# Batch 0's attention with key tiles of 128 instead of 112, its values loaded by all heads at once, in a fused attention and mixer kernel

## The chip, the cores and the metric

The kernel runs on one core of one Trainium2 chip. The metric is the time of one execution on the device, in microseconds, as the median of several.

## The reference, cut to what matters

```python
# q, k, v: (batch 8, heads 12, seq 448, head_dim 64), fp32; tau = 0.1
q_n = q / (norm(q) + 1e-6);  k_n = k / (norm(k) + 1e-6)
attn = softmax(q_n @ k_n.T / tau)             # by head
x = (attn @ v), heads side by side            # (8, 448, 768)
u = x + ((x.T @ U) @ V).T                     # low-rank mixing over seq, rank 32
out = u + relu(u @ w_ch1) @ w_ch2             # 768 -> 3072 -> 768
```

Cosine similarities lie in -1..1, so the kernel leaves out the subtraction of the maximum, and it takes the sum of a softmax row from a column of ones beside v.

## The kernel before: what the change and the argument touch

A planner in Python orders the operations of all engines by estimated times and emits each engine's instructions in that order. Two consequences matter below. In the traces an instruction whose data come late holds up what stands behind it on its engine: in the run with AV late, a square waits 1.46 us for its load, and the exp behind it starts 2.35 us after its score was begun. Any edit may order the rest of the program anew.

Work goes by pairs of heads. For a pair, 448 keys and queries in 4 blocks of 112 rows are squared and reduced (norms), scaled, transposed by TensorE into PSUM, copied to SBUF (`qkT`), multiplied into scores, put through `exp` on ScalarE, and multiplied with v (AV). In batches 1 to 7 keys are tiles of 128, seven for a pair: three of head A, three of head B, and one with 64 rows of each, whose v rows hold zeros for the other head. In batch 0, whose start is in a hurry, keys stay in their blocks of 112:

```python
small = b == 0
rows_ = SCH if small else 128                      # SCH = 112
for m in range(8 if small else 7):
    ... score matmul into sc, 448 columns ...
    exps[m] = ACT exp(attn[0:rows_, m, ...] <- sc)
# AV: 16 matmuls a head either way; batch 0 reads its own value tile raw_v [112, 12, 4, 66]
...
# order of the first loads on GpSimd's queue
load_qk(0, 0, 2); load_qk(0, 2, 4); load_qk(0, 4, 8)
load_v0(0, 4)                                      # 4 loads: heads 0..3
load_qk(0, 8, 12)
load_v0(4, 8); load_v0(8, 12)
load_w1(0, 6); load_w1(6, 12)
```

`raw_v` shares its memory with w2. The two tiles for 128-row values are prepared (ones and zeros) by GpSimd at leisure. ScalarE's instructions are all activations or copies, and VectorE and ScalarE share the copies out of PSUM and the squares, as the planner finds one of them free.

## Time and profile before

| | before |
|---|---|
| time, median of the first 3 runs | 608.21 us (608.17 to 608.47) |
| time of the profiled execution | 607.15 us |
| TensorE busy | 587.7 of 605.0 us |
| TensorE idle before 40 us | 11.4 us |
| first exp, last exp of batch 0 ended | 10.74, 38.05 us |
| first MLP matmul | 39.40 us |

How to read it: from 39.4 us on TensorE is a nearly unbroken queue of matmuls. Before that it waits for the first batch, which ScalarE carries. The lines that show this stand in the prediction.

### The profile page before, as it was taken

The page shows a single profiled execution, that of the slowest core. Times are in us where ns is not written, and L with a number is a line of the kernel's source. Part 1 is how long each engine was busy: PE and PEld are TensorE (multiplying, and loading weights), DVE is VectorE, ACT ScalarE, POOL GpSimd, SP SyncE. Part 2 cuts the span into 40 slices and gives each one's busy share as a digit, 9 for nine tenths or more (in the row PEclk, how much of TensorE's full clock was granted, in tenths as well). Part 3 has the DMA queues.
Part 4 walks back from the last instruction along what each step waited for, and adds up shares of the span by engine and source line. Part 5 has one row for each costly group of instructions (what it writes and reads, how often), then busy time and mean ns, then how long its engine had stood idle before and what let it go on. Part 6 is the DMA issues. An engine that isn't in the chain of part 4 may idle for free.

```text
span 605.0 us, 11545 instructions
## 1 busy us (share of the span) xinstructions
PE 587.7 (97%) x4731; PEld 348.6 (58%) x4731; DVE 295.6 (49%) x703; ACT 281.3 (46%) x606; POOL 120.9 (20%) x191
## 2 busy tenths in 40 slices
PE   4899999999999999999999999999999999999997
PEld 2565665555555665666445665666545666654565
DVE  8979669899998899644711253015300210110011
ACT  6977752488772286327641077506442015014300
POOL 8737234062611626000600000000000000000000
PEclk9999999999999999999999999999999999999999
DMA  9999997999998999724902141030002110310021
GB/s 121 191 206 113 205 197 96 151 150 145 123 113 151 183 153 143 98 67 84 157 0 66 43 89 41 1 93 27 15 1 53 52 40 1 88 43 1 0 53 53
DMA packets 150228, 54.58 MB, mean 90 GB/s; under 512 B 115104, under 2 KB 150176, under 8 KB 150176
## 3 DMA queue, kind: packets, MB, share of 16 engines
q0 software_dynamic: 73408, 25.96, 39.0%
q1 hardware_dynamic: 76704, 27.86, 24.7%
q8 instruction: 37, 0.61, 0.4%
q14 instruction: 15, 0.12, 0.1%
q10 hardware_dynamic: 64, 0.02, 0.0%
HBM read 52.25 MB, written 11.01 MB: 105 GB/s over the span
## 4 chain that ended last, share of the span: by engine, by line
PE 92%; ACT 5%; DVE 1%; DMA 0%; issue 0%; POOL 0%; ACTq 0%; POOLq 0%
PE mm L768 36%; PE mm L734 35%; PE sc L546 9%; PE av L566 7%; ACT attn L551 3%; PE mm L658 1%; ACT qkT L798 1%; PE mm L623 1%; PE tp L371 1%; ACT sq L438 1%; DVE xn L509 1%; PE sc L734 1%; DMA qk_nat<-in_k_dram 0%; ACT uT L798 0%; PE sc L658 0%
## 5 line engine op out<-in xcount | busy, mean ns | idle before, releaser
L734 PE MATMUL mm<-uT,w_sb 128*128 128x512 bf16 (+1 forms) x1134 | 236.5, 353 | 0.0
L768 PE MATMUL mm<-w_sb,relu 128*128 128x384 bf16 (+1 forms) x1368 | 233.4, 323 | 0.3 <-ACT uT L798 0.3
L551 ACT ACTIVATE attn<-sc 128x448 bf16<-128x448 f32 (+1 forms) x342 | 164.3, 565 | 98.0 <-PE av L566 66.4
L768 PEld LDWEIGHTS <-relu 128*128 128x128 bf16 x1368 | 132.6, 98 | 86.7 <-issue 0.9
L734 PEld LDWEIGHTS <-w_sb 128*128 128x128 bf16 x1152 | 112.2, 98 | 101.2 <-issue 0.8
L757 ACT ACTIVATE relu<-mm 128x384 bf16<-128x384 f32 (+1 forms) x172 | 93.9, 546 | 149.3 <-PE mm L734 148.9
L777 DVE TENSOR_TENSOR O_sb<-mm,u_nat 128x384 f32<-128x384 f32 (+1 forms) x57 | 31.1, 549 | 229.4 <-PE mm L768 222.6
L546 PE MATMUL sc<-qkT 128*128 128x448 bf16 (+1 forms) x342 | 105.8, 358 | 4.3 <-DVE qkT L800 1.3
L566 PEld LDWEIGHTS <-attn 128*128 128x128 bf16 (+1 forms) x1536 | 62.7, 98 | 17.7 <-issue 2.3
L409 POOL DMA_DIRECT2D v_nat<-in_v_dram x98 | 63.1, 650 | 35.4 <-DMA w_sb<-in_moe_w_ch_dram 9.7
L444 DVE TENSOR_REDUCE ss<-sq 112x8 f32<-112x512 bf16 x96 | 63.2, 673 | 1.1 <-ACT sq L438 0.7
L509 DVE TENSOR_TENSOR xn<-qk_nat,inv 112x512 bf16<-112x512 bf16 (+1 forms) x97 | 62.4, 676 | 0.3
L566 PE MATMUL av<-v_nat,attn 128*128 128x65 bf16 x1344 | 55.7, 193 | 0.0
L546 PEld LDWEIGHTS <-qkT 128*128 128x128 bf16 (+1 forms) x342 | 31.9, 103 | 24.1 <-issue 7.2
L387 POOL DMA_DIRECT2D qk_nat<-in_q_dram x25 | 17.8, 713 | 134.6 <-DVE xn L509 89.5
L575 DVE TENSOR_TENSOR X_sb<-av,rd 128x256 bf16<-128x256 f32 x96 | 40.2, 419 | 1.7
L573 DVE RECIPROCAL rd<-av 128x4 f32<-128x4 f32 x96 | 17.1, 179 | 38.2 <-PE av L566 37.4
L440 DVE TENSOR_TENSOR sq<-qk_nat 112x512 bf16<-112x512 bf16 x89 | 34.6, 413 | 0.9 <-DMA qk_nat<-in_q_dram 0.8
L672 DVE TENSOR_TENSOR u_nat<-mm,X_sb 128x384 bf16<-128x384 f32 x36 | 19.0, 552 | 11.1 <-PE mm L658 10.9
L371 PE MATMUL tp<-ident,xn 112*128 112x112 bf16 x144 | 11.1, 220 | 8.0 <-DVE xn L509 7.9
L387 POOL DMA_DIRECT2D qk_nat<-in_k_dram x25 | 17.6, 702 | 3.3 <-DMA w_sb<-in_moe_w_ch_dram 3.0
L457 ACT ACTIVATE ln<-ss 112x32 f32<-112x32 f32 (+2 forms) x26 | 6.1, 235 | 23.5 <-DVE ss L444 23.5
(60 smaller groups left out, 174.9 us busy)
## 6 DMA issues: line engine op xcount, KB each, us to landing
qk_nat<-in_q_dram POOLq DMA_DIRECT2D x23, 224.0 KB, 5.7
qk_nat<-in_k_dram POOLq DMA_DIRECT2D x23, 224.0 KB, 6.8
w_sb<-in_moe_w_ch_dram POOLq DMA_DIRECT2D x4, 1152.0 KB, 13.4
w_sb<-in_moe_w_ch_dram POOLq DMA_DIRECT2D x8, 576.0 KB, 16.2
out_dram<-O_sb SPq DMA_DIRECT2D x15, 168.0 KB, 2.2
out_dram<-O_sb SPq DMA_DIRECT2D x16, 144.0 KB, 2.1
out_dram<-O_sb SPq DMA_DIRECT2D x16, 120.0 KB, 2.0
out_dram<-O_sb SPq DMA_DIRECT2D x16, 96.0 KB, 2.2
```

The lines of the kernel that those rows point to most:

```text
L387: ops = [load(lambda i=i, src=src: nc.gpsimd.dma_start(out=ld.tile[:, i, lo:lo + h1 - h0, :], in_=src[b, h0:h1].rearrange("h (s c) d -> s ...
L409: nc.gpsimd.dma_start(out=vb[p0:p0 + s1 - s0, hs, j, 0:D], in_=v[b, hs].rearrange("h (s c) d -> c s h d", c=SC)[c, s0:s1]),
L440: nc.vector.tensor_mul(y, x, x)
L444: lambda i=i, a0=a0, a1=a1, sq=sq: nc.vector.reduce_sum(ss.tile[:, i, a0:a1, :].rearrange("p h c -> p (h c)"), sq.tile[:, 0:a1 - a0, :].re ...
L509: nc.vector.tensor_mul(dst, src, sc)
L546: nc.tensor.matmul(out=sc.tile[0:rows_, 0:S], lhsT=kT[:, rows_ * m:rows_ * (m + 1)], rhs=qkT.tile[:, 8:12, :].rearrange("p c s -> p (c s)" ...
L551: exps[m] = plan.add(Op("ACT", act_t(S), lambda sc=sc, m=m: nc.scalar.activation(out=attn.tile[0:rows_, m, off:off + S], in_=sc.tile[0:row ...
L566: nc.tensor.matmul(out=av.tile[:, t, 0:D + 1], lhsT=attn.tile[0:rows_, m, 128 * t:128 * (t + 1)], rhs=vv[0:rows_, h, j, 0:D + 1], start=(j ...
L575: muls.append(plan.add(Op("DVE", dve_t(256), lambda av=av, rd=rd, h=h: nc.vector.tensor_mul(X.tile[:, :, h * D:(h + 1) * D], av.tile[:, :, ...
L734: o = plan.add(Op("PE", pe_t(n), lambda cc=cc: nc.tensor.matmul(out=mm.tile[:, 0:n], lhsT=w1_sb[:, cc, f * 128:(f + 1) * 128], rhs=uT.tile ...
L757: nc.scalar.activation(out=relu.tile[:, f, 0:n], in_=mm.tile[:, 0:n], func=AF.Relu)
L768: nc.tensor.matmul(out=mm.tile[:, 0:c1 - c0], lhsT=relu.tile[:, f, i * 128:(i + 1) * 128], rhs=w2.tile[:, f, c0:c1], start=(f == 0), stop= ...
```

## The change

Its intent: seven exps for each pair of batch 0 instead of eight, which is 6 of 48, on the engine that carries the chain. Keys come in blocks of 112 from the transposes, so tiles of 128 are put together while they leave PSUM: each of a head's first three blocks is filled up with 16 rows of the fourth, and the 64 rows that are left go to the mixed tile. Values must then lie in tiles of 128 too, and eight loads (six of all heads, two of every second head, each some rows of one block) bring them straight to that layout. w2 gets its own tile.

```diff
-    r_w2 = Ring(... "raw_v" ... then "w2_sb" in the same memory ...)
+    w2_t = const.tile([128, NC, C], BF, name="w2_sb")
+    def load_v0():                                  # all heads
+        for j in range(3):
+            part(0, SCH, slice(0, H, 1), j, j, 0)             # 112 rows of block j
+            part(SCH, 16, slice(0, H, 1), j, 3, 16 * j)       # 16 rows of block 3
+        for hh in range(2):
+            part(64 * hh, 64, slice(hh, H, 2), 3, 3, 48)      # the last 64 rows
...
+    def key_tiles(t_, x, h0, h1):                   # three copies for a block, in place of one
+        return [(full[:, :, :, 0:SCH], x[:, :, 0:3, :]),
+                (full[:, :, :, SCH:128], x[:, :, 3, 0:48] ...),
+                (t_[:, 768 + 64 * h0:768 + 64 * h1] ..., x[:, :, 3, 48:SCH])]
...
-        for m in range(8 if small else 7):
+        for m in (0, 1, 2, 6, 3, 4, 5) if b == 0 else range(7):
...
-    load_v0(0, 4)
+    load_v0()
     ld, ops, _ = load_qk(0, 8, 12)
-    load_v0(4, 8)
-    load_v0(8, 12)
...
-    v_set = [plan.add(Op("POOL", 1.5, lambda t_=t_: set_v(t_)), pool_q) for t_ in v_t]
+    v_set = [fill(lambda: set_v(v_t[0]), 1000, prio=-1.4),           # VectorE, at the start
+             fill(lambda: set_v(v_t[1]), 1000, prio=3, deps=late)]   # VectorE, late
```

## The prediction

> **What bounds the kernel now.** I read the page first: busy shares, slices, the chain that ended last.
>
> ```profile
> PE 587.7 (97%) x4731; PEld 348.6 (58%) x4731; DVE 295.6 (49%) x703; ACT 281.3 (46%) x606; POOL 120.9 (20%) x191
> PE   4899999999999999999999999999999999999997
> ...
> PE 92%; ACT 5%; DVE 1%; DMA 0%; issue 0%; POOL 0%; ACTq 0%; POOLq 0%
> ```
>
> TensorE is busy 97% of 605 us, and only the first slice and the last are short of full. A change confined to batch 0 can therefore gain only in the first 40 us, where TensorE is not yet fed by the MLP; what it gains there should pass through to the end, because everything behind it is a queue of matmuls. Second, the busy time by stretches (columns: TensorE, weight loads, VectorE, ScalarE, GpSimd, then clock, DMA, GB/s):
>
> ```profile
> 4.00:8.00 4.00, 0.34 (x4) 0.32 (x4) 3.52 (x10) 1.35 (x5) 3.92 (x8) 1.00 1.11 135
> 8.00:15.00 7.00, 6.19 (x46) 3.61 (x44) 6.88 (x16) 6.71 (x17) 6.26 (x10) 1.00 1.65 160
> 15.00:17.00 2.00, 1.18 (x25) 1.05 (x23) 1.63 (x6) 2.00 (x6) 1.82 (x4) 1.00 1.94 183
> 17.00:26.50 9.50, 7.68 (x98) 5.41 (x97) 9.40 (x23) 9.50 (x22) 5.58 (x15) 1.00 1.28 184
> 26.50:38.00 11.50, 11.21 (x156) 7.58 (x154) 6.98 (x23) 11.39 (x26) 7.23 (x11) 1.00 1.22 208
> ```
>
> ScalarE is full from 8 to 38 us; VectorE is full with it until 26.5 us and has room only after that. From 4 to 8 us VectorE is the fuller of the two. Third, the chain of waits in that part (start, length, what):
>
> ```profile
> 2.07 2.97 DMA qk_nat<-in_k_dram
> 5.03 0.02 issue
> 5.06 0.64 ACT sq L438
> 5.70 0.02 issue
> 5.72 0.69 DVE ss L444
> ...
> 15.02 0.52 ACT sq L438
> 15.68 0.49 issue
> 16.16 0.30 ACT ln L457
> 16.47 0.52 ACT sq L438
> 17.10 1.31 ACT attn L551 x3
> ...
> 23.38 2.60 ACT attn L551 x6
> 25.98 0.79 ACT qkT L798
> 26.77 5.65 ACT attn L551 x13
> ```
>
> It starts at the key load, goes through VectorE until 7.6 us, and from 8.26 to 32.4 us is almost only ScalarE: exps, key/query copies, squares. After 32.4 us it moves to TensorE, which works on scores, AV and the first stage-0 products in step with the last exps; those run until 38.04 us, and the MLP begins at 39.4 us. So ScalarE's amount of work sets when batch 0 ends, with VectorE and TensorE close behind.
>
> **What the Trainium skill says.** (1) "ScalarE: Activation LUTs", section "What ACT_TABLE_LOAD costs": one ACTIVATE takes a fixed part plus 0.833 ns per element whatever the function, and neighbours overlap by about 93 ns. The trace agrees in slope, with less fixed part between neighbours: six exps of 448 columns in 2.60 us are 0.433 us each, that is 0.373 + 0.060; an 896-column copy takes 0.80 us in the chain, 0.746 + 0.054. Nothing depends on the number of partitions, so 128 rows cost an exp what 112 did. (2) "VectorE: DVE Perf Modes", "The perf-mode tier table": a copy with a PSUM source gets at most two elements a cycle. Agrees: 448 columns took 0.375 us and 896 took 0.594 us, so 0.49 ns per element. (3) Same page, "Zero memsets can be issued as uint32 (trn2)": a memset takes a cycle per element, so words halve it. The trace has 512 words in 0.48 us and 256 in 0.27 us. (4) "DMA: Bandwidth & Descriptors", "Specifications": transfers below 512 B are not at line rate. The value loads move 64 fp32 at a time, 256 B; in the stretch where they dominate (10 to 15 us) the DMAs moved 162 GB/s, against 206 from 35 to 40 us with weights. That fits, without proving the cause.
>
> **The change part by part.**
>
> *Exps.* Eight tiles of 112 keys become seven of 128 per pair: 48 exps become 42. 6 x 0.433 = 2.6 us less on ScalarE. Six score matmuls go too (about 0.19 us each in the chain, 1.1 us), but on TensorE, which is not the limit before 32 us; they only keep its part of the tail from becoming one. AV stays at 16 matmuls per head.
>
> *Copies.* A key block leaves PSUM in three copies instead of one: 672 + 96 + 128 columns for 896, 336 + 48 + 64 for 448. Same elements, two fixed parts more: 2 x 0.055 = 0.11 us on ScalarE for each block. There are seven key blocks (two for the first pair). Before, ScalarE made four of the five large copies, and both of pair 0's key copies: six of seven. Then 6 x 0.11 = 0.65 us more. On VectorE the fixed part read from (2), 0.375 - 448 x 0.49 ns = 0.155, less the 0.08 by which neighbours' spans overlap, gives 0.15 us for each block there; one or two, 0.15 to 0.3 us. ScalarE's net is then 2.6 - 0.65 = 1.95 us.
>
> *The fill of v.* The 0.14 us memset of the old value tile goes; VectorE now prepares the first v tile with five word memsets of 36, 6, 198, 6 and 198 columns. With 0.06 + 0.82 ns per word (line through the 256 and 512 word memsets): 0.09 + 2 x 0.065 + 2 x 0.22 = 0.66 us, plus some 0.1 us at each change of partition range (after the 128-row memset at 1.52 us, 0.27 long, the next begins at 1.89): about 0.9 us. Net +0.75 us, and by its priority it stands ahead of the first square. Today the fills end at about 4.37 us and that square starts at 4.29, just when its query load lands (issue 1.29 + 3.0). It would start at 5.05, end with its reduction at about 6.05, and the keys' reduction, which starts at 5.72 today, would start at 6.05. VectorE holds the chain from there until 7.6 us, so +0.35 us for everything behind. The second v tile is filled late, where VectorE has 4.5 us of room; GpSimd loses 2.3 us of fills, but it then waits for the last U load until 25.99 us, so nothing starts earlier there.
>
> *Value loads first.* Twelve loads become eight, all before the queries and keys of heads 8 to 11. These were issued at 8.74 and 9.43 us and landed at about 14.1 and 16 us; ScalarE squared them at 14.86 and 16.30 us, in the gap while pair 1's keys were not ready. Now 0.69 MB (bf16) of values go ahead of their 0.46 MB. After the keys of heads 4 to 7 land at 11.3 us (4.73 + 6.6), 0.69 MB at 165 GB/s (the rate of 10 to 16 us) take 4.2 us: values at about 15.5 us, then queries at about 17 and keys at 18.3 us. So the two squares of 0.52 us cannot fill the gap before 17 us. ScalarE idles for part of it and does them later, among the exps. Pair 1's copies start a little sooner in their absence, so I charge 0.8 us rather than 1.04. The first AV moves from 13.15 to about 15.7 us; both attn buffers are still free for pairs 0 and 1, so no exp waits. Statistics of heads 8 to 11, whose logarithm runs at 22.5 us now, may slip by 0.8 us to 23.3, with pair 4's keys in SBUF at about 27 us; by my sum ScalarE is then still in pairs 2 and 3, so this costs nothing.
>
> *w2 in its own tile.* Its first load would come behind batch 1's value loads, still being issued at 50 us, long after the old values are freed at 38.9 us. No change.
>
> Sum for the end of batch 0: -1.95 + 0.35 + 0.8 = -0.8 us. The MLP's first matmul at about 38.6 instead of 39.4 us. Behind it, batch 1's squares are released by batch 0's last product, so they shift too. A little more is possible in the tail: 25 exps from 26.50 to 38.04 us take 0.462 each and not 0.433, 0.7 us of waiting on TensorE's order, which fewer scores ease by perhaps 0.2 us. Total -1.0 us: 607.2 us.
>
> **The rivals.** *A: ScalarE's saving arrives whole, 605.8 to 606.3 us.* The fills find room before the loads land, VectorE takes the late squares. For: the first query load lands only at 4.3 us. Against: fills already end then, and VectorE is 99% full from 17 to 26.5 us. *B: the wait moves to the loads, 608 to 609 us.* If heads 8 to 11 land after 20 us, or all-head value loads land at 17 us, statistics become late and pairs 4 and 5 stall the exps; the GB/s columns speak for the danger, the spare time of pairs 2 and 3 against it. *C: VectorE becomes the limit, about 608 us.* It loses 0.75 at the start, gains the copies, and is already full until 26.5 us; then a shorter ScalarE list merely waits for keys. *D: the reordered instruction stream shifts waits in batch 1*, where TensorE idles 0.43 us (45 to 50) and 0.56 us (55 to 60): up to 0.5 us either way.
>
> **Range and chances.** Best case is 2.6 us plus the tail, about 605.4; B and C together give 609. Runs agree to 0.3 us. I take 607.2 us, 605.8 to 608.6 for 8 in 10. Two per cent is 12 us, more than the whole first gap of TensorE (11.4 us idle before 40 us): 0.01 faster, 0.98 same, 0.01 slower.
>
> **What would show it.** 42 exps in batch 0, still near 0.433 us each; seven key blocks of three copies, about 0.11 us longer per block on ScalarE; the first VectorE square near 5.05 us and the first exp near 11.1 instead of 10.74 us; ScalarE with a hole between 15 and 17 us, and the squares of heads 8 to 11 after 17 us; last exp near 37.2 us; first MLP matmul near 38.6 us; TensorE behind it unchanged in busy time. It is wrong if ScalarE has holes after 24 us (B or C), if the first square still starts at 4.3 us (A), or if the MLP starts as predicted and the end does not follow (D).

## The result, and the profile after

| | before | after |
|---|---|---|
| first comparison, median | 608.19 us (4 runs, 607.26 to 608.47) | 607.20 us (4 runs, 606.58 to 607.85) |
| ratio, 95% interval | | 0.9987 (0.9969 to 1.0004) |
| second comparison, another time, median | 607.12 us (9 runs, 607.01 to 607.94) | 607.40 us (5 runs, 607.17 to 607.67) |
| ratio, 95% interval | | 1.0002 (0.9989 to 1.0014) |

A ratio compares mean times, so it is not quite the ratio of the medians. The result is correct. It is within noise of no change: the first comparison says 0.8 us less with an interval from 1.9 us less to 0.2 us more, the second 0.1 us more (0.7 less to 0.9 more). The predicted 607.2 us was met to the digit, which says little, as the kernel before itself moved by 1.1 us between the two comparisons. What has to be explained is the sum: 2 us of ScalarE's work are gone, and hardly any of it arrives.

The stretches of the changed kernel, the same borders and columns as in the prediction (TensorE, weight loads, VectorE, ScalarE, GpSimd, clock, DMA, GB/s):

```profile
4.00:8.00 4.00, 0.07 (x2) 0.08 (x3) 3.83 (x10) 1.46 (x5) 3.92 (x8) 1.00 1.17 144
8.00:15.00 7.00, 5.03 (x24) 2.05 (x25) 6.89 (x17) 6.31 (x19) 6.21 (x10) 1.00 1.92 141
15.00:17.00 2.00, 2.00 (x34) 2.00 (x33) 1.31 (x5) 1.52 (x6) 0.88 (x2) 1.00 1.44 206
17.00:26.50 9.50, 7.80 (x98) 4.92 (x96) 9.33 (x24) 9.04 (x25) 0.97 (x1) 1.00 1.20 205
26.50:38.00 11.50, 10.96 (x180) 7.91 (x177) 8.66 (x32) 10.87 (x26) 7.33 (x11) 1.00 1.13 173
```

Before, ScalarE had 0.29 us of idle time from 8 to 15 us and none from 15 to 26.5 us; now it has 0.69 us from 8 to 15 us, 0.48 us from 15 to 17 us and 0.46 us from 17 to 26.5 us. TensorE, with 1.18 us in the stretch from 15 to 17 us before, is full there. TensorE's timeline of the changed kernel (start, length, what, how many):

```profile
14.61 0.93 PE L365 MATMUL tp<-ident,xn 112*128 112x112 bf16 x8 [0.60 <-DVE xn L527]
15.33 0.59 PE L583 MATMUL av<-v_nat,attn 128*128 128x65 bf16 x7
15.73 0.56 PE L365 MATMUL tp<-ident,xn 112*128 112x112 bf16 x4
16.09 1.58 PE L583 MATMUL av<-v_nat,attn 128*128 128x65 bf16 x25
17.48 2.42 PE L563 MATMUL sc<-qkT 128*128 128x448 bf16 x6
```

Pair 1's keys are transposed at 14.61 us. Then the AV of pair 0, all 32 matmuls, stands ahead of pair 1's scores, which start only at 17.48 us. In the kernel before AV came earlier, in the gaps while pair 0's exps ran, because it needed only the values of heads 0 to 3:

```profile
13.15 0.43 PE L566 MATMUL av<-raw_v,attn 112*128 112x65 bf16 x4
13.39 0.60 PE L546 MATMUL sc<-qkT 128*112 128x448 bf16 x1
13.79 0.87 PE L566 MATMUL av<-raw_v,attn 112*128 112x65 bf16 x12
14.46 0.62 PE L371 MATMUL tp<-ident,xn 112*128 112x112 bf16 x8
...
15.21 0.57 PE L566 MATMUL av<-raw_v,attn 112*128 112x65 bf16 x13
16.61 0.73 PE L546 MATMUL sc<-qkT 128*112 128x448 bf16 x3 [0.82 <-DVE qkT L800]
```

ScalarE's side of it, changed kernel: the gap before pair 1's first exp is put down to the score.

```profile
15.57 1.03 ACT L815 COPY qkT<-tp 128x672 bf16<-128x672 bf16 x3 [0.33 <-PE tp L365]
...
18.08 1.42 ACT L568 ACTIVATE attn<-sc 128x448 bf16<-128x448 f32 x3 [0.46 <-PE sc L563]
```

The copy of a key block is the group of three that starts at 15.57 us; the next two blocks, in the chain of waits of the same kernel, are one entry, and so are eight exps:

```profile
21.74 1.84 ACT qkT L815 x6
...
24.69 3.47 ACT attn L568 x8
```

1.84 us for two blocks is 0.92 us each, against 0.80 us before; 3.47 us for eight exps is 0.434 us each, as before with 112 rows.

From several profiles the following moments were read in the trace, in us. "Pair 1" is its first exp, "batch 1" the time from the first MLP matmul to batch 1's first score, "rest" the time from the first MLP matmul to the start of the last one.

| kernel | first exp | pair 1 | last exp ends | first MLP matmul | batch 1 | rest |
|---|---|---|---|---|---|---|
| before, first profile | 10.74 | 17.00 | 38.05 | 39.40 | 9.07 | 561.82 |
| before, again | 10.62 | 17.20 | 38.27 | 39.63 | 9.07 | 561.80 |
| after, first profile | 11.44 | 18.08 | 37.14 | 38.58 | 9.39 | 562.22 |
| after, again | 11.45 | 18.42 | 37.51 | 38.96 | 9.39 | 562.43 |

Read along a line, the changed kernel loses 0.7 to 0.8 us up to the first exp and 0.4 us more up to pair 1, wins 2.0 us from there to the last exp (21.05 and 21.07 us before, 19.07 and 19.09 after), enters the MLP 0.7 to 0.8 us sooner, and gives back 0.4 to 0.6 us behind that. At the last matmul 0.4 us or nothing is left. The experiments take these stretches one by one.

### The profile page after: what moved, and what is told of

Its sections match the earlier page's. It is cut to its first block, busy times and chain, and to the rows that moved or that the text cites. A ratio compares the mean times of both kernels' runs of the same rounds, so it can differ in the third digit from the quotient of the medians.

```text
span 604.8 us, 11544 instructions
## 1 busy us (share of the span) xinstructions
PE 586.1 (97%) x4725; PEld 346.8 (57%) x4725; DVE 296.0 (49%) x714; ACT 279.5 (46%) x612; POOL 115.4 (19%) x177
## 4 chain that ended last, share of the span: by engine, by line
PE 92%; ACT 5%; DVE 2%; issue 0%; ACTq 0%
PE mm L785 36%; PE mm L751 35%; PE sc L563 9%; PE av L583 8%; ACT attn L568 3%; PE mm L675 1%; ACT qkT L815 1%; PE tp L365 1%; PE mm L640 1%; DVE ss L452 1%; PE sc L751 1%; DVE xn L527 0%; PE sc L675 0%; ACT uT L815 0%; DVE xn L820 0%
## 5 line engine op out<-in xcount | busy, mean ns | idle before, releaser
L568 ACT ACTIVATE attn<-sc 128x448 bf16<-128x448 f32 x336 | 161.0, 565 | 88.8 <-PE av L583 57.4
L774 ACT ACTIVATE relu<-mm 128x512 bf16<-128x512 f32 (+1 forms) x169 | 92.4, 547 | 149.2 <-PE mm L751 148.9
L563 PE MATMUL sc<-qkT 128*128 128x448 bf16 x336 | 103.4, 358 | 3.9 <-ACT attn L568 1.9
L583 PEld LDWEIGHTS <-attn 128*128 128x128 bf16 x1536 | 62.7, 98 | 16.0 <-DVE xn L527 0.8
L583 PE MATMUL av<-v_nat,attn 128*128 128x65 bf16 x1536 | 66.6, 194 | 0.2 <-DVE X_sb L592 0.2
L563 PEld LDWEIGHTS <-qkT 128*128 128x128 bf16 x336 | 29.8, 98 | 24.2 <-issue 8.0
```

Source lines behind the costliest of these rows:

```text
L563: nc.tensor.matmul(out=sc.tile[:, 0:S], lhsT=kT[:, 128 * m:128 * (m + 1)], rhs=qkT.tile[:, 8:12, :].rearrange("p c s -> p (c s)"), start=T ...
L568: exps[m] = plan.add(Op("ACT", act_t(S), lambda sc=sc, m=m: nc.scalar.activation(out=attn.tile[:, m, off:off + S], in_=sc.tile[:, 0:S], fu ...
L583: nc.tensor.matmul(out=av.tile[:, t, 0:D + 1], lhsT=attn.tile[:, m, 128 * t:128 * (t + 1)], rhs=v_t[b % 2][:, h, j, 0:D + 1], start=(j == ...
L774: nc.scalar.activation(out=relu.tile[:, f, 0:n], in_=mm.tile[:, 0:n], func=AF.Relu)
```

## The experiments

Twelve runs, in three sessions. The first two were on one chip, and nine of the ten runs of the kernel before that the second is compared with are those of the first; the third was on another chip, with eleven runs of its own.

### The changed kernel once more, and the kernel before once more

No edit.

> The changed kernel once more, to size the noise. My theory: the gain of the profile (last exp of batch 0 at 37.0 us against 38.0, first MLP matmul at 38.6 against 39.4) is real and repeats within 0.15 us; the time is 0.5 to 1.0 us under the kernel before. Rival (the difference of the first measurement is noise of single executions, which spread over 1.3 us): the interval of the ratio spans 1.000 evenly and the landmarks move by 0.3 us or more.

> The kernel before once more, for its landmarks on this chip: first exp 10.7 us, pair 1's first exp 17.0, last exp of batch 0 38.0, first MLP matmul 39.4, last MLP matmul 561.8 us after the first. If the landmarks of one program move by more than 0.2 us between chips, the 0.8 us gain of the changed kernel's first profile is not safe; I expect less than 0.2 us, since the values land long before the AV that uses them.

Measured: the times of the second comparison above, and for the single look at the kernel before 607.34 us. The landmarks of both programs moved by up to 0.38 us, more than I had allowed for the changed kernel and a little more than for the kernel before. The gain at the first MLP matmul repeats (0.82 and 0.67 us); the gain in time doesn't. So the difference inside batch 0 is real, and the rival was right that it isn't to be seen in the time.

### The first fill moved from VectorE to ScalarE

```diff
-    v_set = [fill(lambda: set_v(v_t[0]), 1000, prio=-1.4),
+    v_set = [plan.add(Op("ACT", 1.5, lambda: set_v_act(v_t[0]), deps=[attn_set[0]], prio=-3)),
```

`set_v_act` writes the same ones and zeros by five ScalarE copies, before its first square.

> The first v tile is filled by five ScalarE copies in its idle time from 2.0 to 4.9 us, in place of five VectorE memsets in front of the first square. My theory (VectorE holds the chain until the first exp): the first square starts at about 4.3 us instead of 4.9, the first exp about 0.3 to 0.6 us sooner than 11.4, the first MLP matmul about 0.3 us sooner than 38.6. Rival (VectorE is full until 26 us anyway, or ScalarE's later holes swallow it): first exp sooner, first MLP matmul unchanged within 0.15 us.

Measured: median 606.94 us, ratio 0.9994 (0.9979 to 1.0010). The first square started at 4.45 us instead of 4.88, but the first exp stayed at 11.41 us and the first MLP matmul at 38.88 (38.96 in the run beside it). The expectation failed at its second step. The fills were not what made the first exp late.

### The epsilon added as a tensor

In the changed kernel the two small additions ahead of pair 0's scaling took 0.43 and 0.62 us, and were 0.32 and 0.17 us before. VectorE's timeline of the changed kernel, then GpSimd's value loads beside it, as merged by the view:

```profile
6.47 0.43 DVE L471 TENSOR_SCALAR ln<-ln 112x8 f32<-112x8 f32 x1
6.94 0.20 DVE L473 RECIPROCAL inv<-ln 112x8 f32<-112x8 f32 x1
7.17 0.69 DVE L527 TENSOR_TENSOR xn<-qk_nat,inv 112x512 bf16<-112x512 bf16 x1
7.78 0.62 DVE L471 TENSOR_SCALAR ln<-ln 112x8 f32<-112x8 f32 x1
8.44 0.20 DVE L473 RECIPROCAL inv<-ln 112x8 f32<-112x8 f32 x1
8.68 0.76 DVE L527 TENSOR_TENSOR xn<-qk_nat,inv 112x256 bf16<-112x256 bf16 x2
```

```profile
5.98 5.74 POOL L420 DMA_DIRECT2D v_nat<-in_v_dram  x8
```

The eight issues within that entry start at 5.98, 6.92, 7.46, 8.39, 8.93, 9.86, 10.39 and 11.08 us: those with 112 rows take 0.95 us, those with 16 rows 0.55 us (0.70 us each before). The additions end at 6.90 and 8.41 us, each just when an issue of 0.95 us ends.

```diff
-            nv.tile[:, w, 0:g, :], nv.tile[:, w, 0:g, :], EPS)          # tensor_scalar_add
+            nv.tile[:, w, 0:g, :], nv.tile[:, w, 0:g, :],
+            eps_t[:, 0:1, 0:1].unsqueeze(3).to_broadcast([...]))        # tensor_add
```

> The small additions of the epsilon on VectorE (0.43 and 0.63 us in the changed kernel, each ending with a GpSimd load issue, against 0.17 us where no issue was in the way) become additions of two tensors, which should not have to wait for GpSimd's port. My theory: each takes under 0.25 us, the first exp comes about 0.5 us sooner than 11.4 us, the first MLP matmul 0.2 to 0.5 us sooner. Rival (their length is not the port but a wait for ScalarE's result): they stay at 0.4 to 0.6 us and the first exp stays.

Measured: 607.76 us, ratio 1.0009 (0.9995 to 1.0023). The two additions took 0.17 and 0.16 us, under the same issues, and keys were scaled at 7.98 us instead of 8.68, pair 0's scores started at 9.83 us instead of 10.35. That part of my theory holds. The Trainium skill has it in "SBUF — State Buffer", section "Who interferes with whom": a VectorE instruction in a 2-port mode takes an exclusive lock on a port pair that GpSimd's descriptor writing also needs, and whichever comes second waits for the whole instruction of the other; a tensor_tensor has no 2-port mode. The trace agrees, with waits of up to 0.46 us (0.62 less 0.16). All fourteen traces show it, and they show a limit. Of these tensor_scalar additions, 22 began 0.30 to 0.45 us after the start of an issue that had at least 0.2 us to go; all 22 ended within 0.03 us of its end. But the 32 that began within 0.22 us of an issue's start took 0.15 to 0.18 us, as if nothing were in the way. None of the 15 additions of two tensors that began under an issue took over 0.2 us.

Yet the first exp did not come sooner, but at 11.60 us. ScalarE's timeline of this run:

```profile
9.75 0.69 ACT L818 COPY qkT<-tp 128x336 bf16<-128x336 bf16 x3
10.96 0.63 ACT L448 ACTIVATE sq<-qk_nat 112x512 bf16<-112x512 bf16 x1 [0.52 <-DMA qk_nat<-in_q_dram]
11.50 0.20 ACT L467 ACTIVATE ln<-ss 112x16 f32<-112x16 f32 x1
11.60 0.53 ACT L571 ACTIVATE attn<-sc 128x448 bf16<-128x448 f32 x1
```

A square of heads 4 to 7 is ahead of the first exp on ScalarE, and its queries landed only at 10.87 us; in the first profile of the changed kernel they landed at 9.58 us. The wait taken away was followed at once by a wait for a load. And the MLP started at 40.47 us, 1.5 us later than in the run beside it, though nothing that this edit touches is there. That points to the loads, and the table after the next runs takes it up.

### Queries and keys of heads 8 to 11 ahead of the values

```diff
-    load_v0()
     ld, ops, _ = load_qk(0, 8, 12)
+    load_v0()
```

> Queries and keys of heads 8 to 11 are loaded ahead of the values. My theory (the value loads in front of them cost about 0.8 us, because ScalarE has a hole of about 0.9 us in all before pair 1's exps at 18.1 us): they land by 14 us, their squares fill the hole, the first AV moves to about 17.5 us, the first MLP matmul comes 0.3 to 0.8 us sooner than 38.6. Rival (pair 1's exps wait for VectorE's and TensorE's work, not for ScalarE): squares move forward, pair 1's first exp stays near 18 us and the MLP starts as before or later, since AV now comes late and stands in the way of scores.

Measured: 609.4 us, ratio 1.0034 (1.0020 to 1.0048), slower. Both theories have a part in it. The queries and keys landed at 12.4 and 13.8 us, the hole was filled, and pair 1's first exp came at 16.92 us instead of 18.42, so VectorE was not what held it at 18 us. The edit does not part loads from order, though: the planner also put three of pair 1's scores ahead of AV. The first exp of all came at 10.95 us instead of 11.44 to 11.45: with other loads issued in that time the two additions took 0.16 and 0.17 us, though the fills were still on VectorE. But the last value landed at 19.7 us, and the AV that waits for it stood between pair 1's third score and its fourth. TensorE's timeline of this run:

```profile
16.35 1.28 PE L563 MATMUL sc<-qkT 128*128 128x448 bf16 x3 [0.93 <-ACT ln L465]
17.43 0.58 PE L583 MATMUL av<-v_nat,attn 128*128 128x65 bf16 x2
19.16 0.24 PE L583 MATMUL av<-v_nat,attn 128*128 128x65 bf16 x1 [1.16 <-DMA v_nat<-in_v_dram]
19.58 0.44 PE L583 MATMUL av<-v_nat,attn 128*128 128x65 bf16 x5 [0.18 <-DMA v_nat<-in_v_dram]
19.82 0.56 PE L563 MATMUL sc<-qkT 128*128 128x448 bf16 x1
```

The first MLP matmul came at 40.95 us. My prediction had said of the late AV that no exp waits for it. Here ScalarE waits 1.58 us for the score behind it. In the second profile of the changed kernel itself the same wait is in the chain of waits:

```profile
10.42 5.43 DMA v_nat<-in_v_dram
15.84 0.04 issue
15.88 0.38 PE av L583 x4
16.26 0.38 PE tp L365 x4
16.64 1.38 PE av L583 x25
18.01 0.39 PE sc L563
```

### AV of pair 0 behind pair 1's first scores

The planner was told that values land 3 us later than it had assumed. That alone changes TensorE's order; the order of loads is the same.

```diff
-                n * (0.0055 if hs.step == 2 else 0.011)))
+                n * (0.0055 if hs.step == 2 else 0.011), late=5.0))
```

> The instruction order alone: TensorE's AV of pair 0 stands behind pair 1's transposes and its first four scores, not in front of them; all loads and all work are as in the changed kernel. New theory (the predicted cost of the value loads is not a hole for lack of squares: pair 1's scores stand in TensorE's queue behind an AV that waits for the last value load, at 15.8 us, and then takes 1.4 us): pair 1's first exp moves from 18.1 to 18.4 us forward to 16.6 to 17.0, the first MLP matmul from 38.6 to 39.0 forward to about 37.6. Rival (ScalarE's hole comes from VectorE, whose key and query copies are late): pair 1's first exp stays at 18 us and the MLP start stays within 0.2 us.

Measured: median 606.46 us (605.74 to 607.91), ratio 0.9983 (0.9967 to 0.9998), the only interval that lies below 1, by a hair. That is weak evidence: it is one of eleven intervals, and the plain mean of these four runs over that of the ten of the kernel before is 0.9988. The profiled execution was the slowest of the four, so its trace shows the bad case. In it pair 1's scores did start at 16.46 us, as the new theory wanted, but its first exp only at 18.81 us: a square of heads 8 to 11 stood ahead of it on ScalarE and waited 1.46 us for queries that landed at 18.07 us. So neither expectation about the exp could be met in this trace, and the MLP began at 41.01 us, where 37.6 was expected. The order is confirmed as a cause for the scores; what the exp then meets is another load.

### Query copy of batch 1's first pair bound to VectorE

```diff
-                    [o], [qkT], [xn], 1, "ACT/DVE", ...
+                    [o], [qkT], [xn], 1, "DVE" if b == 1 and p == 0 and b0 == 8 else "ACT/DVE", ...
```

The reason to try it is in the chain of waits where batch 1 begins. The kernel before, then the changed one:

```profile
45.62 2.50 DVE xn L509 x4
48.12 0.31 DVE qkT L800
48.43 0.04 issue
48.48 0.54 PE sc L546 x2
```

```profile
46.11 0.41 PE tp L365 x8
46.52 0.02 issue
46.54 1.39 ACT qkT L815 x2
47.93 0.04 issue
47.98 0.54 PE sc L563 x2
```

The changed kernel has its transposes 0.84 us sooner and its score only 0.50 us sooner, since both copies are on ScalarE, one behind the other.

> The query copy of batch 1's first pair is bound to VectorE, as it was in the kernel before; in the changed kernel ScalarE makes the key and the query copy one after the other (1.4 us) before batch 1's first score. Theory (0.3 us of the gain is given back there, because the order was planned anew): batch 1's first score comes 9.1 us after the first MLP matmul instead of 9.4, and the last MLP matmul about 0.3 us sooner after the first than 562.2 to 562.4. Rival (TensorE has other work to do meanwhile): the first score moves, the end does not.

Measured: 606.56 us, ratio 0.9989 (0.9976 to 1.0003). Batch 1's first score came 9.25 us after the first MLP matmul, half of the 0.3 us that I wanted; the rest of the kernel took 561.67 us, against 562.2 to 562.4 in the changed kernel and 561.8 before. So the 0.4 us behind the MLP's start went away in this run. That the copy is the cause isn't shown: the score moved by 0.14 us and the end by more, and in the run with AV late the rest took only 561.37 us with the score still at 9.39 us. Any new order of the plan may move this stretch by as much; what in it costs the time stays open.

### One copy for each key block (wrong result)

```diff
-    key_tiles(t_, x, b0 // 4, b1 // 4) if b == 0 and b0 < 8 else [(t_[:, b0:b1, :], x)]
+    [(t_[:, b0:b1, :], x)]
```

> Each key block of batch 0 leaves PSUM in one copy, which puts keys at wrong places: a wrong result on purpose, same work otherwise. Theory (two more copies cost 0.11 us for each block on ScalarE, six of seven blocks are there): the key copies of 896 columns take 0.80 us of ScalarE in place of 0.91, and the last exp of batch 0 comes 0.4 to 0.7 us sooner than the 37.1 to 37.5 of the changed kernel. Rival (the copies lie in ScalarE's holes): it moves by less than 0.2 us.

Measured: 607.98 us, one run; the result was wrong as meant. Two blocks took 1.71 us as a pair in place of 2.00 us in ScalarE's timeline (1.84 us in the chain, without the overlapped start), so three copies cost about 0.14 us more for a block, where 0.11 was predicted. The last exp ended at 38.42 us, later than in the changed kernel and not sooner. The sizes are confirmed; the moment of the end says nothing here, since the loads were late in this execution too.

### What the late executions have in common

Seven profiles have the changed kernel's order of loads. From each trace, the landing of the queries of heads 4 to 7, of queries and keys of heads 8 to 11, and two moments, in us:

| kernel | q of 4-7 | q, k of 8-11 | pair 1 | last exp ends |
|---|---|---|---|---|
| after, again | 9.03 | 16.87, 17.84 | 18.42 | 37.51 |
| fill on ScalarE | 9.36 | 16.86, 17.94 | 18.37 | 37.44 |
| after, first | 9.58 | 16.79, 18.09 | 18.08 | 37.14 |
| one copy | 10.47 | 17.89, 19.02 | 18.91 | 38.42 |
| AV late | 10.64 | 18.07, 20.23 | 18.81 | 39.56 |
| batch 1 copy | 10.86 | 18.19, 20.28 | 19.36 | 38.42 |
| epsilon as tensor | 10.87 | 18.43, 19.95 | 19.82 | 39.03 |
| before (two profiles) | 10.12, 9.56 | 14.18, 15.64 and 14.61, 15.80 | 17.00, 17.20 | 38.05, 38.27 |

There are two groups. GpSimd's timeline tells them apart; first the changed kernel, then the run with the batch 1 copy, which has the same instructions there:

```profile
8.93 2.80 POOL L420 DMA_DIRECT2D v_nat<-in_v_dram  x4
12.47 0.73 POOL L387 DMA_DIRECT2D qk_nat<-in_q_dram  x1 [0.75 <-DMA v_nat<-in_v_dram]
```

```profile
8.92 1.48 POOL L420 DMA_DIRECT2D v_nat<-in_v_dram  x2
11.14 0.65 POOL L420 DMA_DIRECT2D v_nat<-in_v_dram  x1 [0.74 <-DMA qk_nat<-in_q_dram]
12.23 0.64 POOL L420 DMA_DIRECT2D v_nat<-in_v_dram  x1 [0.44 <-DMA qk_nat<-in_k_dram]
13.72 0.73 POOL L387 DMA_DIRECT2D qk_nat<-in_q_dram  x1 [0.84 <-DMA v_nat<-in_v_dram]
```

GpSimd's seventh value load is issued only when the queries of heads 4 to 7 have landed, the eighth when their keys have. The semaphores in the trace's records say why, and it is the program's doing: its loads on GpSimd use eight semaphores in turn (99 to 106), so from the ninth on each waits for the load eight places before it. Where that load is late, the issue follows 0.28 us after its landing, in both kernels. Where the queries of heads 4 to 7 land at 9.0 to 9.6 us, no value load waits (only the next load does, 0.37 to 0.75 us, for the first values); where they land after 10.4 us, each issue behind them slips, queries and keys of heads 8 to 11 land 0.9 to 2.4 us later, and batch 0 ends 0.9 to 2.4 us later, behind the kernel before. The edits of these runs have a part in that, but the run with the batch 1 copy has the changed kernel's order of instructions on TensorE, ScalarE and VectorE up to 47 us, so its 1.3 us at the end of batch 0 against the first profile (38.42 and 37.14 us) come with the loads alone. The kernel before has those two loads behind only four small value loads, and in both of its profiles they had landed by 15.8 us. Why the queries of heads 4 to 7 land early or late in a program whose first six loads are the same, the runs don't show.

### The change's order of loads, on the kernel before

```diff
     load_v0(0, 4)
-    ld, ops, _ = load_qk(0, 8, 12)
-    stats(0, 8, 12, ld, ops, 0)
     load_v0(4, 8)
     load_v0(8, 12)
+    ...                          # every pair's AV now waits for all twelve value loads
+    ld, ops, _ = load_qk(0, 8, 12)
+    stats(0, 8, 12, ld, ops, 0)
```

> The kernel before with the change's order of loads alone: all twelve value loads ahead of the queries and keys of heads 8 to 11, and pair 0's AV waits for all of them; eight tiles of 112 keys, one copy for a block and the fills stay as they were. Theory (the changed kernel's 2 us of saved ScalarE work is given back by the landing of these loads): queries and keys of heads 8 to 11 land at 18 to 20 us instead of 14.2 to 15.8, the last exp of batch 0 moves from 38.1 to 38.3 us to 39.0 or later, and the time is 0.7 to 1.5 us over the kernel before. Rival (the loads are harmless, the changed kernel loses its gain by its copies and by the order planned anew): last exp within 0.3 us of 38.2, time unchanged.

Measured: 611.63 us, ratio 1.0079 (1.0059 to 1.0098). The last exp ended at 41.84 us and the MLP began at 43.19 us, 3.6 to 3.8 us later than in the kernel before. Some 0.6 us of that was lost before the first exp (11.36 us), where the very first keys landed at 5.74 us instead of 5.0 in this execution. Queries and keys of heads 8 to 11 landed at 20.4 and 21.6 us. The direction is the theory's, the size near three times the upper end of my range (4.1 us by the medians): twelve issues of 0.7 us with two waits between them put the last two loads off to 15.1 us. ScalarE's timeline of this run has the gap and the load it is put down to:

```profile
17.39 1.41 ACT L551 ACTIVATE attn<-sc 112x448 bf16<-112x448 f32 x3 [0.32 <-PE sc L546]
20.40 0.63 ACT L438 ACTIVATE sq<-qk_nat 112x512 bf16<-112x512 bf16 x1 [1.59 <-DMA qk_nat<-in_q_dram]
20.94 1.40 ACT L551 ACTIVATE attn<-sc 112x448 bf16<-112x448 f32 x3
```

So the order of loads is able to take away more than the seven exps bring. In the changed kernel it costs less, since the queries of heads 8 to 11 are issued at 12.1 to 13.8 us there. The edit also makes AV wait for all twelve value loads, the last of which landed at 18.8 us; how much of the cost is that, no run parts.

### Values in two groups, and three combinations of the edits

```diff
-    load_v0()
+    load_v0(0, 4)                     # 8 loads: heads 0 to 3, in tiles of 128
     ld, ops, _ = load_qk(0, 8, 12)
     late = stats(0, 8, 12, ld, ops, 0)
+    load_v0(4, H)                     # 8 loads: heads 4 to 11
```

> The changed kernel with the values in two groups: heads 0 to 3 (eight small loads), then queries and keys of heads 8 to 11, then values of heads 4 to 11 (eight loads). Theory: values of pair 0 land by about 14 us and the queries of heads 8 to 11 by about 16, pair 1's first exp comes at about 17 us instead of 18.1 to 19.4, the last exp of batch 0 at 36.3 to 36.9 us instead of 37.1 to 39.6, and the time is about 1 to 1.5 us under the kernel before. Rival (GpSimd's sixteen issues at 0.55 to 0.95 us each, in place of eight, delay the later values so that pairs 2 to 5 wait): no better than the changed kernel.

Measured: 607.97 us (606.81 to 608.18), ratio 1.0001 (0.9988 to 1.0014). Pair 0's values landed by 14.0 us, as wanted, and the queries of heads 8 to 11 at 16.1 us. But their keys landed at 17.75 us, no sooner than in the changed kernel: the eight small loads were through on GpSimd at 11.96 us, no sooner than the large ones (11.72), because it waited here, 0.59 and 0.57 us, for the loads of heads 4 to 7 (queries 9.93, keys 11.09 us). Pair 1's first exp came at 17.98 us and the last exp ended at 38.45 us. Two squares of heads 8 to 11 now stood on ScalarE ahead of pair 1's exps, the first waiting 1.43 us for its queries. The theory failed here; the rival's reason, too many issues, fits what GpSimd did, though the pairs that waited were not only the late ones.

The next run adds the fill on ScalarE and the batch 1 copy on VectorE to the split values:

> The split values, the first fill on ScalarE in its idle time, and batch 1's first query copy on VectorE. Theory: last exp of batch 0 at 36.0 to 36.8 us, batch 1's first score 9.2 us after the first MLP matmul, time 1.2 to 2.0 us under the kernel before. Rival: as the changed kernel, within 0.5 us of the kernel before.

Measured: median 606.72 us (605.52 to 608.97), ratio 0.9987 (0.9970 to 1.0004). In the profile pair 1 began at 17.58 us, the last exp ended at 38.85 us, the MLP began at 40.30 us and batch 1's first score came 9.36 us later, all short of the theory. But this profile is not a fair one: TensorE's granted clock was 0.5 from 23.14 to 26.55 us, inside batch 0. In the other thirteen profiles the records of the clock (which begin at 14.6 to 23.9 us) show less than 1 only after 603 us. The six runs fall into two groups by their mean clock: 605.52, 605.70 and 606.04 us at 0.999 to 1.000, but 607.41, 607.75 and 608.97 us at 0.993 to 0.997. The eleven runs of the kernel before, at 0.999 to 1.000, took 607.17 to 608.45 us. So the 1.2 to 2.0 us of the theory may be there at the full clock. Three runs picked afterwards don't show it, and in the section before this one three of four runs were at 0.997 and two of them took as long as the one at 1.000. A repeat with traces at the full clock would have settled it.

The last has the epsilon as a tensor as well:

> The same with the epsilon added as a second tensor, so that VectorE does not wait for GpSimd's load issues. Theory: first exp before 10.9 us, the rest as the run with split values, fill and copy or up to 0.4 us sooner. Rival (the first exps wait for a square of heads 4 to 7, which waits for its load, as in the run of that change alone): first exp stays at 11.0 us or later and nothing is gained.

Measured: median 607.02 us (606.44 to 607.23), ratio 0.9987 (0.9974 to 1.0000). Its first exp did come at 10.71 us, as soon as in the kernel before, so the first exp's delay can be taken away when the loads don't interfere. The fills have no visible share in it: with the values split it came at 10.95 us, with the fill moved as well at 10.94 us. The small value loads, with issues of 0.5 to 0.7 us, took off 0.5 us, the epsilon as a tensor 0.23 us. Pair 1 still began at 18.40 us, after queries and keys that landed at 16.5 and 18.0 us, and the MLP at 39.85 us. The gain of the first stretch was lost in the second. In both runs the rest of the kernel took 561.5 us, 0.3 us less than before, which is the only gain that their profiles show. By the ratios of all runs, none of the versions beats the kernel before by more than 0.2%.

## Why the prediction was right or wrong, point by point

The time lay in the range, and the sum for the first MLP matmul (-0.8 us) was what the two profiles of the changed kernel show (-0.8 and -0.7). The terms are a different matter.

1. **Exps and copies, -1.95 us: right.** 42 exps, 0.434 us each with 128 rows. Three copies cost 0.11 to 0.14 us more for a block. From pair 1's first exp to the last one the kernel needs 2.0 us less, in the first two profiles of each kernel alike. This stretch has five of the six saved exps (5 x 0.433 = 2.2 us) and three blocks copied by ScalarE (0.3 us).

2. **The fills, +0.35 us at the front: wrong in cause, and too small.** The first exp came 0.70 us later (0.83 in the second pair of profiles). The fills moved the first square by 0.59 us, but the keys' reduction only by 0.15 us (from 5.72 to 5.87 us, as two reductions of 0.6 us from 5.27 us on), and without them the first exp stayed where it was. The additions of the epsilon, stretched from 0.32 and 0.17 us to 0.43 and 0.62 us by GpSimd's longer load issues, make up the rest. Since they end with the issues, the fills ahead of them don't matter. The step that failed is "so +0.35 us for everything behind": it counted VectorE's own instructions and not what else holds its port.

3. **Values first, +0.8 us: right in size, right in cause by half.** The landing times were good: values at about 15.5, queries at 17 and keys at 18.3 us were predicted, and 15.8, 16.8 and 18.1 us measured. From the first exp to pair 1's first exp takes 6.64 us instead of 6.26, although there is one exp of 0.43 us fewer, so the cost is 0.8 us. ScalarE, never idle in this stretch before, is idle for 0.93 us of it in the first profile and 1.25 us in the second. The predicted hole is one half of that: 0.33 and 0.32 us end with pair 1's transposes, where a square stood before, and 0.15 and 0.22 us with a square whose queries land at 16.8 us. The other half, 0.46 and 0.72 us, ends with pair 1's first score. Here the step that failed is "both attn buffers are still free for pairs 0 and 1, so no exp waits". I looked at the buffers and not at the order: AV of pair 0 stands in TensorE's list ahead of pair 1's scores, so that the exps of pair 1 wait for 1.4 us of AV matmuls and, in the second profile, for a value load that lands at 15.84 us. The square that was to come later stands in ScalarE's list ahead of pair 1's exps and makes them wait for its own load.

4. **No change of the rest: wrong by 0.4 to 0.6 us.** Rival D named it, at up to 0.5 us either way, and I gave it no share in the middle value. Its sign came true: the MLP started as predicted and the end did not follow. Both copies of batch 1's first pair went to ScalarE in the order planned anew. Binding one to VectorE took this off in one profile, with an interval of the time that still touches 1, but the run with AV late lost it too without that edit. The cause stays open.

5. **Rival B, loads that become the wait.** I gave it 608 to 609 us and took it for unlikely while loads land as estimated. They do so in some executions. In four of seven profiles with this order they landed 1 to 2 us later, and batch 0 then ended later than before the change. Rival C, VectorE as the limit, was seen for the front: in the first profile of the changed kernel the chain of waits stays on VectorE until pair 1's keys are scaled at 14.56 us, where before it left VectorE at 7.6 us. In the second it comes from the values' load instead. Behind pair 1's first exp, VectorE was not the limit in the first profile: from 18.08 to 32.56 us its chain is ScalarE's.

6. **GpSimd.** "Nothing starts earlier there" holds, but the last U load landed at 27.90 us instead of 25.88, and batch 1's first queries were issued at 28.59 us instead of 26.65. I had not priced that. No run shows a cost from it.

The predicted figure thus came out by two terms that were right and by errors that largely cancelled: the front was 0.35 us too cheap, the tail's 0.2 us of further gain is in the 2.0 us, and the part behind the MLP's start was missing. The range of 1.4 us either side was wide enough for all of it. That the figure was met is luck. "Runs agree to 0.3 us" was too narrow as well: four runs of the changed kernel spread over 1.3 us. And TensorE is short of full in the second slice too (8 tenths), which changes nothing here.

What stays open: what takes 0.4 to 0.6 us behind the MLP's start, why the first loads land in two groups of times, and how often each occurs without a profile. The spread of single runs (605.7 to 607.9 us for one program) has the size of the difference, which fits, but no trace exists of the fast ones.

## What to carry to other kernels

When work is taken off the engine that carries the chain, look next at what the saving needs in exchange: here all heads' values at once, ahead of loads that the chain waits for. In a kernel whose engines run fixed lists, ask of each late instruction not only who needs its result but what stands behind it on its engine, and of each early load whether the plan still holds when it lands a microsecond later. Count how many loads the program lets be under way: here the ninth waits for the first. A hit on the total of a prediction is no proof of its terms; moments read inside the trace are.

## What the Trainium skill lacked or had wrong

- "DMA: Bandwidth & Descriptors", section "Anatomy of one DMA — SWDGE (gpsimd) path", calls the generation of descriptors "small, variable" and does not say how it grows with a load. Issuing a value load of 112 rows by 12 heads took GpSimd 0.95 us, one of 16 rows 0.55 us, and the ends of VectorE's waits fall on the ends of these issues.
- "SBUF — State Buffer", section "Who interferes with whom", was right in the main and decided a case: additions of 112 x 8 elements took 0.43 and 0.62 us as tensor_scalar and 0.17 and 0.16 us as tensor_tensor, under the same load issues. It says that the loser waits for the whole instruction; a load issue of GpSimd did not hold up the 32 additions that began within its first 0.22 us (0.15 to 0.18 us each).
- No page says how far the landing of the same first loads spreads between executions: the queries of heads 4 to 7, fifth in the queue, landed at 9.0 to 10.9 us.
